# Down-sampled and local attention with a gated feed-forward layer on one core: first loads put in another order, small copies and products merged, and the list of steps drawn anew

## The chip, the cores and the metric

One Trainium2 chip, of which the program uses one core. The metric is device time in microseconds from start to end of the program, as the median over runs.

## The reference

For 8 batches of 8 heads, with 576 positions and 64 values a head, the reference makes two attentions and adds them: one over positions averaged by fours and repeated four times, and one over a band of seven keys. The sum, as 4608 tokens of 512 values, goes through a feed-forward layer with a gate.

```python
q_d, k_d, v_d = (t.reshape(B, H, S // 4, 4, D).mean(axis=3) for t in (q, k, v))
out_up = np.repeat(sm_attn(q_d, k_d, v_d), 4, axis=2)
mask = np.abs(pos[:, None] - pos[None, :]) < 4
attn = softmax(np.where(mask, scale * q @ k.transpose(0, 1, 3, 2), -1e9))
x = (out_up + attn @ v).transpose(0, 2, 1, 3).reshape(B * S, H * D)
y = (np.maximum(x @ w_gate, 0) * (x @ w_val)) @ w_out
```

## The kernel before

Two heads make a pair; there are 32 pairs, four to a batch. The tokens are cut in 9 chunks of 512. As soon as the pairs of a chunk's batch are done, the feed-forward products of that chunk run between the steps of the next pairs. Many of these products are made by schemes with seven products of half-size blocks in place of eight, with their sums on DVE.

PSUM is one tile, `ps`, of eight banks of 512 numbers. Each step names its bank.

The order of everything is written by hand: `SEQ` (L18) is a string of 2329 steps, and the loop at the end issues them one by one. Each engine runs its own instructions strictly in the order in which the list issues them; between engines, waits are put in from what each instruction reads and writes. A range of `ps` that an access spans counts as read, also where the access leaves banks out. So the list is at once the order of PE, ACT, DVE, POOL and SP.

A step is written kind/pair/arguments/bank. Those that matter here:

- `loadq`, `loadk`, `loadv` issue a pair's loads on POOL (L458, DMA rows at L467; L495, rows at L517). `cast` turns q of pair 0 to f16 on ACT.
- `tr/p/i/b` transposes a third of q and k of pair p on PE into bank b (`emit_flip2`, L547, matmuls L553, of half the array's width); it leaves 2 x 96 columns of each position and 2 x 48 of pooled ones there.
- `ev/p/i0X/b` copies the positions to `qkT` and `ev/p/i1X/b` the pooled columns to `qkd` (`emit_flipped`, L577, rows at L589), on ACT (X is A) or DVE (V).
- `s1` makes the scores on PE (L650 pooled, L661 in the band). They need `qkd` and `qkT`. `ed` and `ex` are their exponentials on ACT (L685, L671), `ma` the band's mask on DVE (L677).
- `vd`, `vc` pool v on PE (L631) and copy it on ACT (L640).
- `sd`, `su` are the products with v on PE (L698 and L710), `rd`, `ru` reciprocals of the sums of the exponentials on DVE (L722, L735), `td`, `tu` the normalising products on DVE (L727, L741): `tu` has two a pair, for three of the six blocks of 96 positions each.
- `xp`, `xe` transpose the result on PE (L928, L930) and copy it to `xT` (L940).
- `warm` and `brief` are matmuls on zeros that fill PE's time (L1115, L1125).
- From pair 4 on, `den` and `num` (L751, L760 and L772, L781, half the array's width) take the place of `sd`, `su` and what follows; from pair 8 on they are written `o/a...`, `o/b...`.
- `hg`, `hv` are whole-array products of the feed-forward layer (L945), `p`, `up`, `sq` blocks of the seven-product schemes (L1030, L1289, L1193), `next`, `sum`, `sumhi` their sums (L1024), `gate` and `gt` the gate (L957, L1384).
- POOL also adds parts of v for the later pairs (L602, L610).

Before the list starts, q of pair 0 is loaded through SP, the constants too, and twelve wide matmuls on zeros run on PE.

Of the kernel before, what the change touches and what calls it, by code (L numbers as in the profile page):

```python
# [12 lines left out]
ALU = mybir.AluOpType  # L13
# [5 lines left out]
qk/a0/0@6 cast tr/0/0/2 ev/0/00A/2 loadk/0 loadv/0 pads tr/0/1/3 ev/0/10A/3 ev/0/11A/3 tr/0/2/4 vd/0/6 ev/0/01A/2  # L19
loadq/1 loadk/1 loadk/3 ev/0/21V/4 loadv/1 tr/1/0/7 ev/0/20V/4 s1/0/2 loadq/2 loadk/2 vc/0/6 ev/1/00A/7 tr/1/2/1  # L20
tr/1/1/0 ev/1/01A/7 loadv/2 loadv/3 ed/0/2 warm/5/6 sd/0/6 loadq/3 loadk/4 wv/0 loadq/4 ex/0/0/2 brief/16/2 ev/1/21V/1
ev/1/20V/1 wg/0 loadk/5 ev/1/10A/0 loadv/4 rd/0/6 ma/0/0 ev/1/11A/0 loadk/6 s1/1/0 loadq/5 td/0/6 ex/0/1/2 ma/0/1
warm/2/7 ex/1/0/0 ma/1/0 su/0/4 ru/0/4 ed/1/0 vd/1/6 tr/2/0/0 ex/1/1/0 tr/2/2/3 tu/0/1/4 tu/0/0/4 tr/2/1/2 vc/1/6
ev/2/21V/3 ev/2/20V/3 ev/2/01A/0 ev/2/00A/0 ma/1/1 ev/2/11A/2 xp/0/1/5 xp/0/0/4 sd/1/6 xe/0/1V/5 ev/2/10A/2 s1/2/0
xe/0/0A/4 ex/2/0/0 ed/2/0 su/1/4 rd/1/6 td/1/6 warm/5/7 warm/1/7 vd/2/6 tr/3/0/0 ex/2/1/0 ma/2/0 ru/1/4 tu/1/1/4
tu/1/0/4 ma/2/1 tr/3/1/2 ev/3/00A/0 ev/3/01A/0 tr/3/2/3 ev/3/20V/3 ev/3/21V/3 warm/3/7 xp/1/1/5 xe/1/1V/5 ev/3/11A/2
vc/2/6 xp/1/0/4 sd/2/6 ev/3/10A/2 xe/1/0A/4 rd/2/6 td/2/6 s1/3/0 su/2/4 vd/3/6 ex/3/0/0 wg/1 loadv/5 ru/2/4 tu/2/1/4
tu/2/0/4 wv/1 hv/0/0/7 hv/0/1/7 ed/3/0 ex/3/1/0 tr/4/0/0 warm/4/1 ev/4/01A/0 wg/2 vc/3/6 xp/2/0/4 ev/4/00A/0 xe/2/0A/4
xp/2/1/5 ma/3/0 hv/1/0/1 loadq/6 loadk/8 loadk/7 loadv/6 ma/3/1 loadq/7 sd/3/6 hv/1/1/1 wv/2 xe/2/1V/5 su/3/4 rd/3/6
tr/4/2/3 tr/4/1/2 td/3/6 ev/4/11A/2 ev/4/10A/2 loadv/7 ru/3/4 tu/3/0/4 tu/3/1/4 hg/0/0/6 hg/0/1/6 hv/0/2/7 hg/1/0/0  # L30
wv/3 ones/6 ev/4/21V/3 loadq/8 ev/4/20V/3 wg/3 xp/3/1/5 xp/3/0/4 hv/1/2/1 hg/0/2/6 wo/1 xe/3/1V/5 wo/0 wo/2 xe/3/0A/4
s1/4/2 ex/4/0/2 hg/0/3/6 relu/0/6 hv/1/3/1 hv/0/3/7 hg/1/1/0 hg/1/2/0 hg/1/3/0 vd/4/6 ed/4/2 tr/5/0/2 tr/5/1/3
ex/4/1/2 tr/5/2/4 ev/5/01A/2 relu/1/0 vc/4/6 ev/5/10A/3 ev/5/11A/3 ev/5/00A/2 gate/0/7 ma/4/0 ma/4/1 hv/2/*/7 hg/2/*/6
relu/2/6 ev/5/20V/4 ev/5/21V/4 gate/1/1 den/4/1/5 den/4/0/4 ln/4 inv gate/2/7 num/4/1/3 num/4/0/2 xn/2 vd/5/1 hg/3/*/0
vc/5/1 s1/5/4 ex/5/0/4 hv/3/*/1 ex/5/1/4 ed/5/4 hg/4/*/2 hg/5/*/6 relu/3/0 relu/4/2 hv/4/*/3 ma/5/0 ma/5/1 tr/6/0/4
gate/3/1 xsum/4 gate/4/3 relu/5/6 tr/6/1/0 ev/6/00A/4 ev/6/11V/0 ev/6/01V/4 ones/4 num/5/0/2 den/5/1/5 tr/6/2/1
kk/a0/1@6 ev/6/10A/0 wo/3 num/5/1/3 qk/a2/0@6 qk/b1/0@0 den/5/0/4 kk/a1/1@6 const/0 const/1 v4/a/0@1 ln/4 inv
ev/6/21V/1 ev/6/20V/1 qk/a2/1@6 hv/5/*/7 gate/5/7 qk/b3/1@6 vd/6/1 vc/6/1 tr/7/1/0 s1/6/4 hg/7/*/1 xn/2 ev/7/11V/0
hg/8/*/2 hv/7/*/3 v/a/0@6 ex/6/1/4 ex/6/0/4 ma/6/0 ma/6/1 xsum/5 sum/2/0@1 ed/6/4 hg/6/*/7 v/a/1@6 relu/8/2 relu/7/1
gate/7/3 ev/7/10V/0 den/6/1/5 tr/7/2/1 tr/7/0/6 den/6/0/4 hv/8/*/0 relu/6/7 hv/6/*/7 num/6/0/2 ev/7/01V/6 gate/8/0  # L40
num/6/1/3 tr/8/2/0 ev/7/20A/1 loadv/8 qk/b0/0@0 qk/b1/1@0 qk/a0/1@0 qk/a3/1@0 qk/b3/0@0 qk/b2/0@0 qk/a2/1@0 qk/a1/0@1
qk/b0/1@0 qk/a1/1@0 v/a/1@0 v/b/0@0 qk/b2/0@1 qk/b2/1@0 qk/b3/1@0 gate/6/7 ln/4 inv ev/7/00A/6 ev/7/21A/1 s1/7/4
# [36 lines left out]
o/b10/0@2 o/b11/0@2 vh/7.1/0@2 next/2/0@2 gt/7.1.1/0@2 sq/2.2.0.6/1@2 up/0.1/1@2 ln/b0/0@2 inv/b/0@2 xn/b0/0@2
# [1538 lines left out]
```

## Time and profile before

| | us |
|---|---|
| median of 3 runs | 335.33 |
| the runs | 335.18, 335.33, 338.43 |
| the profiled execution | 334.61 |
| its span | 332.7 |
| PE's granted clock in it | 1.0 |

The span runs from the first to the last instruction of the profile. The rest of the profiled execution's time, 1.9 us, lies around it. In the rows, a start is in microseconds from the span's start, followed by the busy time of the group of like instructions; a matmul's end is modelled, so the starts are what tells how fast PE goes.

### The profile page before, as it was taken

How to read it: one execution, taken by the hardware profiler on the slowest of the kernel's cores; microseconds unless marked ns; L12 is line 12 of the kernel's file. 1: busy time of each engine (PE TensorE's matmuls, PEld its weight loads, DVE VectorE, ACT ScalarE, POOL GpSimd, SP SyncE). 2: the span in 40 equal slices, each digit the busy share in tenths (PEclk: the TensorE clock that was granted, in tenths of full speed). 3: DMA queues.
4: the chain of work that ended last, by engine and by line, in shares of the span. 5: the costliest groups of instructions: out<-in, count | busy, mean ns of one | idle time of the engine just before them, and what ended most of it. 6: DMA issues, size and time to landing. Idle time of an engine off the chain costs nothing.

```text
span 332.7 us, 9158 instructions
## 1 busy us (share of the span) xinstructions
PE 327.0 (98%) x3456; PEld 244.1 (73%) x3456; DVE 287.2 (86%) x574; ACT 268.3 (81%) x649; POOL 183.8 (55%) x268
## 2 busy tenths in 40 slices
PE   7999999999999999999999999999999999999996
PEld 3876556666577787778687868786878678888875
DVE  6795779999997989999999989979998998788792
ACT  4968887789988989899879989898889548787852
POOL 8864845928989788867974998845520000000000
PEclk9999999999999999999999999999999999999999
DMA  9999999999999999999999999999200102003024
GB/s 143 173 188 215 183 203 165 135 168 160 169 179 142 210 114 224 119 210 102 218 134 186 121 214 136 210 133 173 39 32 3 63 2 97 1 19 111 2 58 133
DMA packets 151808, 43.96 MB, mean 132 GB/s; under 512 B 136556, under 2 KB 146452, under 8 KB 151764
## 3 DMA queue, kind: packets, MB, share of 16 engines
q0 software_dynamic: 113344, 19.51, 79.1%
q1 hardware_dynamic: 38308, 23.83, 33.9%
q8 instruction: 27, 0.44, 0.6%
q14 instruction: 17, 0.14, 0.1%
q10 hardware_dynamic: 112, 0.04, 0.1%
HBM read 46.63 MB, written 9.44 MB: 169 GB/s over the span
## 4 chain that ended last, share of the span: by engine, by line
PE 95%; DMA 2%; DVE 1%; POOL 1%; issue 1%; ACT 1%; DVEq 0%; POOLq 0%
PE ps L945 30%; PE ps L1289 27%; PE ps L1193 18%; PE ps L1030 3%; PE ps L873 2%; PE ps L553 2%; PE ps L846 2%; PE ps L893 2%; DMA qk<-in_q_dram 2%; PE ps L888 1%; PE ps L842 1%; PE ps L631 1%; PE ps L661 1%; PE ps L650 1%; PE ps L751 1%; PE ps L772 1%
## 5 line engine op out<-in xcount | busy, mean ns | idle before, releaser
L945 PE MATMUL ps<-xT,wv_sb 128*128 128x512 f16 x352 | 90.0, 380 | 0.0
L945 PEld LDWEIGHTS <-wv_sb 128*128 128x128 f16 x352 | 32.7, 98 | 25.9
L472 POOL DMA_DIRECT2D qk<-in_k_dram x46 | 33.6, 734 | 16.7 <-DMA qkT<-qk 12.3
L1384 DVE SCALAR_TENSOR_TENSOR gT<-r,ps 128x512 f16<-128x512 f16 x55 | 37.3, 681 | 4.7 <-PE ps L945 3.8
L1289 PE MATMUL ps<-xT,qk 128*128 128x256 f16 x240 | 41.3, 272 | 0.0
L472 POOL DMA_DIRECT2D qk<-in_q_dram x46 | 34.0, 741 | 11.2 <-DMA qkT<-qk 4.6
L1289 PE MATMUL ps<-xT,wg_sb 128*128 128x256 f16 x180 | 33.8, 272 | 0.2 <-DVE xT L1307 0.2
L1300 ACT COPY ps<-ps 128x256 f32<-128x256 f32 x80 | 28.6, 365 | 5.7 <-PE ps L1289 4.8
L490 POOL DMA_DIRECT2D vw<-in_v_dram x40 | 28.9, 732 | 4.3 <-DMA qk<-in_q_dram 4.2
L540 DVE TENSOR_REDUCE qkd<-qkT 128x288 f16<-128x1152 f16 x23 | 30.8, 1341 | 0.0
L1204 ACT COPY ps<-ps 128x256 f32<-128x256 f32 x54 | 19.7, 370 | 12.7 <-PE ps L1193 11.4
L1289 PEld LDWEIGHTS <-qk 128*128 128x128 f16 x240 | 22.4, 97 | 7.4 <-issue 0.5
L610 POOL TENSOR_TENSOR vd<-v 48x192 f16<-48x192 f32 x40 | 25.8, 644 | 1.7
L945 PE MATMUL ps<-xT,wg_sb 128*128 128x512 f16 x104 | 26.6, 380 | 0.0
L1305 ACT CAST r<-ps 128x256 f16<-128x256 f32 x55 | 20.0, 372 | 7.8 <-PE ps L1289 6.8
L1289 PEld LDWEIGHTS <-xo 128*128 128x128 f16 x240 | 22.8, 98 | 3.3
L602 POOL TENSOR_TENSOR v<-v 112x384 f32<-112x384 f32 (+1 forms) x21 | 21.4, 1020 | 6.1 <-DMA v<-in_v_dram 5.6
L1289 PE MATMUL ps<-wt,xo 128*128 128x256 f16 x180 | 24.4, 273 | 0.0
L923 ACT ACTIVATE rden<-rden 128x720 f32<-128x720 f32 x28 | 22.5, 804 | 0.7
L957 DVE TENSOR_TENSOR gT<-r,ps 128x512 f16<-128x512 f16 x24 | 16.2, 680 | 6.7 <-ACT r L954 4.0
L1289 PEld LDWEIGHTS <-wg_sb 128*128 128x128 f16 x180 | 16.4, 97 | 6.5 <-issue 0.6
L1307 DVE TENSOR_TENSOR r<-ps,xT 128x256 f16<-128x256 f32 x44 | 17.3, 419 | 3.2 <-PE ps L1289 2.2
(175 smaller groups left out, 873.7 us busy)
## 6 DMA issues: line engine op xcount, KB each, us to landing
out_dram<-y_sb SPq DMA_DIRECT2D x24, 256.0 KB, 4.3
v<-in_v_dram SPq DMA_DIRECT2D x20, 192.0 KB, 5.3
qk<-in_q_dram POOLq DMA_DIRECT2D x46, 72.0 KB, 5.7
qk<-in_k_dram POOLq DMA_DIRECT2D x46, 72.0 KB, 6.0
vw<-in_v_dram POOLq DMA_DIRECT2D x38, 80.0 KB, 4.6
v<-in_v_dram SPq DMA_DIRECT2D x20, 144.0 KB, 5.5
out_dram<-y_sb SPq DMA_DIRECT2D x22, 128.0 KB, 1.8
vw<-in_v_dram POOLq DMA_DIRECT2D x12, 168.0 KB, 6.4
```

What stands on the lines that cost most here:

```text
L472: nc.gpsimd.dma_start(dst.rearrange("p (j h d) -> p j h d", h=2, d=64)[:, :, hh, :], _dap(src, off + hh * S * D, [[D, 96], [NQ * D, NB], [ ...
L490: nc.gpsimd.dma_start(t[lo : lo + 64, j0:j1, lo : lo + 64], _dap(v, base + j0 * QB * D, [[D, 64], [QB * D, j1 - j0], [1, D]]),)
L540: nc.vector.tensor_reduce(out=qkd[hp % 2].rearrange("p i t -> p (i t)"), in_=qkT[hp % 4][:, 0 : 2 * S].rearrange("p (t f) -> p t f", f=4), ...
L602: nc.gpsimd.tensor_tensor(out=m, in0=t[:, :, 0:128], in1=t[:, :, 128:256], op=ALU.add)
L610: nc.gpsimd.tensor_tensor(out=vp[hp % 3][lo : lo + 48, :, lo : lo + 64], in0=m[:, :, 0:64], in1=m[:, :, 64:128], op=ALU.add)
L923: nc.scalar.activation(out=rden, in_=rden, func=AF.Exp, scale=-1.0)
L945: nc.tensor.matmul(out=out, lhsT=w[:, kk, bass.ts(jj, 128)], rhs=xT[:, kk, c * TCH : (c + 1) * TCH], start=(kk == 0), stop=(kk == 3),)
L1193: nc.tensor.matmul(out=out, lhsT=self.left[i][t], rhs=self.right[i][t], start=(i == 1 and t == 0), stop=(t == n - 1), skip_group_check=True,)
L1289: nc.tensor.matmul(out=out, lhsT=self.left[i - 1][k], rhs=self.right[i - 1][k], start=(i == 1 and k == 0), stop=(k == n - 1), skip_group_c ...
L1300: nc.scalar.copy(out=o, in_=x)
L1305: nc.scalar.copy(out=o, in_=self.d if i == 11 else self.a)
L1384: lambda c, jj, b, t: nc.vector.scalar_tensor_tensor(out=gT[c % 2][:, jj, :], in0=tg[t], scalar=0.0, in1=ps[:, b, :], op0=ALU.max, op1=ALU ...
```

## The change

Three things are done to the steps, and the list is written anew around them.

The first loads: q of pair 1 goes ahead of v of pair 0, and the loads of pairs 1 to 3 follow in the order q, k, v (k of pair 3 stood among those of pair 1). `vd/0`, which reads v of pair 0, now stands behind the scores of pair 0.

The pooled copies on ACT of pairs 1, 2 and 3, `ev/p/01A` and `ev/p/11A`, become one, `eq/p/b0/b1`, which reads two banks in one access. In pair 1 the banks of the two first flips are swapped to 0 and 7.

The normalising products of pairs 0, 1 and 2, `tu/p/0` and `tu/p/1`, become one, `ta/p`, over all six blocks.

Matmuls, loads and what is computed are the same. The list has 2323 steps.

```diff
 SEQ = """
-qk/a0/0@6 cast tr/0/0/2 ev/0/00A/2 loadk/0 loadv/0 pads tr/0/1/3 ev/0/10A/3 ev/0/11A/3 tr/0/2/4 vd/0/6 ev/0/01A/2
-loadq/1 loadk/1 loadk/3 ev/0/21V/4 loadv/1 tr/1/0/7 ev/0/20V/4 s1/0/2 loadq/2 loadk/2 vc/0/6 ev/1/00A/7 tr/1/2/1
-tr/1/1/0 ev/1/01A/7 loadv/2 loadv/3 ed/0/2 warm/5/6 sd/0/6 loadq/3 loadk/4 wv/0 loadq/4 ex/0/0/2 brief/16/2 ev/1/21V/1
-ev/1/20V/1 wg/0 loadk/5 ev/1/10A/0 loadv/4 rd/0/6 ma/0/0 ev/1/11A/0 loadk/6 s1/1/0 loadq/5 td/0/6 ex/0/1/2 ma/0/1
+qk/a0/0@6 cast tr/0/0/2 ev/0/00A/2 loadk/0 loadq/1 pads tr/0/1/3 ev/0/10A/3 ev/0/11A/3 tr/0/2/4 ev/0/01A/2 loadv/0
+loadk/1 loadv/1 ev/0/21V/4 loadq/2 tr/1/0/0 ev/0/20V/4 s1/0/2 vd/0/6 loadk/2 loadv/2 ev/1/00A/0 vc/0/6 tr/1/2/1
+tr/1/1/7 loadq/3 loadk/3 ed/0/2 warm/5/6 sd/0/6 loadv/3 wv/0 loadk/4 loadq/4 ex/0/0/2 brief/16/2 ev/1/21V/1 ev/1/20V/1
+wg/0 loadk/5 ev/1/10A/7 loadv/4 rd/0/6 ma/0/0 eq/1/0/7 loadk/6 s1/1/0 loadq/5 td/0/6 ex/0/1/2 ma/0/1 warm/2/7 ex/1/0/0
...
-den/7/0/4 gate/10/6 zs/0.1/0@1 den/7/1/5 ln/4 inv next/0/1@0 num/7/1/7 tr/8/0/1 num/7/0/6 gate/11/0 next/1/1@0
...
+gate/9/1 next/0/1@0 wt/0 zero/b/6 vc/7/4 den/7/0/4 relu/11/7 num/7/1/7 den/7/1/5 next/1/1@0 gate/11/0 sumhi/0/0@1
+zero/k/0 p/1/0@1 num/7/0/6 ln/4 inv wt/1 tr/8/0/1 tr/8/1/0 p/2/0@1 p/5/0@1 keep/1/0@1 ev/8/01A/1 ev/8/10A/0
...
+    def emit_pooled_two(hp, b0, b1):
+        o = qkd[hp % 2].rearrange("p i t -> p (i t)")[:, 0:192].rearrange("p (b n t) -> p b n t", b=2, n=2)
+        nc.scalar.copy(out=o, in_=_sap(flat, (0, 128), 512 * b0 + 96, [[512 * (b1 - b0), 2], [240, 2], [1, 48]]))
...
+    def emit_tu_all(hp, bank):
+        nc.vector.tensor_tensor(
+            out=xo[hp % 3][:, 0:NB, :].rearrange("p j (h d) -> p h j d", h=2),
+            in0=_sap(ps, (0, 96), 512 * bank, [[513, 2], [65, NB], [1, 64]]),
+            in1=_sap(ru[hp % 2], (0, 96), 0, [[NB, 2], [1, NB], [0, 64]]),
+            op=ALU.mult,
+        )
...
+        "eq": emit_pooled_two,
...
+        "ta": emit_tu_all,
```

POOL's first loads, in the order before (`qk16_1` and `vw_1` are q and k, and v, of pair 1; the line of a row is that of the load):

```order
L467 DMA qk16_0_72<-in_k_dram 96x6x128
L517 DMA vw_0_82<-in_v_dram 112x12x64
L467 DMA qk16_1_73<-in_q_dram 96x6x128
L467 DMA qk16_1_73<-in_k_dram 96x6x128
L467 DMA qk16_3_75<-in_k_dram 96x6x128
L517 DMA vw_1_83<-in_v_dram 112x12x64
L467 DMA qk16_2_74<-in_q_dram 96x6x128
L467 DMA qk16_2_74<-in_k_dram 96x6x128
L517 DMA vw_2_84<-in_v_dram 112x12x64
L517 DMA vw_3_85<-in_v_dram 112x12x64
L467 DMA qk16_3_75<-in_q_dram 96x6x128
```

And now, from the same place (the lines of after are one lower here):

```order
L466 DMA qk16_0_72<-in_k_dram 96x6x128
L466 DMA qk16_1_73<-in_q_dram 96x6x128
L516 DMA vw_0_82<-in_v_dram 112x12x64
L466 DMA qk16_1_73<-in_k_dram 96x6x128
L516 DMA vw_1_83<-in_v_dram 112x12x64
L466 DMA qk16_2_74<-in_q_dram 96x6x128
L466 DMA qk16_2_74<-in_k_dram 96x6x128
L516 DMA vw_2_84<-in_v_dram 112x12x64
L466 DMA qk16_3_75<-in_q_dram 96x6x128
L466 DMA qk16_3_75<-in_k_dram 96x6x128
L516 DMA vw_3_85<-in_v_dram 112x12x64
```

q of pair 1 and v of pair 0 change places; k of pair 1 is the fourth in both. k of pair 3 goes from fifth to tenth.

ACT from the copy of pair 0's pooled v on, before, with the engines that a row waits for in brackets (`qkT_90` and `qkd_94` belong to pair 1, L685 and L671 are `ed` and `ex`):

```order
L640 CAST vd_96<-ps 72x2x2x64 [waits PE_49]
L589 CAST qkT_90<-ps 128x384 [waits PE_49]
L589 CAST qkd_94<-ps 128x96
L685 ACTIVATE att<-ps 72x2x2x144 [waits DVE_49,PE_49]
L671 ACTIVATE att<-ps 112x2x288
L589 CAST qkT_90<-ps 128x384 [waits PE_49]
L589 CAST qkd_94<-ps 128x96
L671 ACTIVATE att<-ps 112x2x288
L671 ACTIVATE att<-ps 112x2x288 [waits DVE_49,PE_49]
```

And now (L595 is `eq`):

```order
L588 CAST qkT_90<-ps 128x384 [waits PE_49]
L643 CAST vd_96<-ps 72x2x2x64 [waits PE_49]
L688 ACTIVATE att<-ps 72x2x2x144 [waits DVE_49]
L674 ACTIVATE att<-ps 112x2x288
L588 CAST qkT_90<-ps 128x384 [waits PE_49]
L595 CAST qkd_94<-ps 128x192 [waits DVE_49,PE_49]
L674 ACTIVATE att<-ps 112x2x288
L674 ACTIVATE att<-ps 112x2x288 [waits PE_49]
```

The first copy of 96 columns is gone, the second is 192 wide and has waits of its own, on DVE and on PE; the copy of pair 0's pooled v moved behind pair 1's first.

446 lines of the change are left out of this document (222 added, 224 removed).

## The prediction

> **What bounds the kernel now.** I read the page's head first, then the waits of PE, then the stretches of the start and of one busy stage.
>
> ```profile
> span 332.7 us, 9158 instructions
> PE 327.0 (98%) x3456; PEld 244.1 (73%) x3456; DVE 287.2 (86%) x574; ACT 268.3 (81%) x649; POOL 183.8 (55%) x268
> PE 95%; DMA 2%; DVE 1%; POOL 1%; issue 1%; ACT 1%; DVEq 0%; POOLq 0%
> ...
> PE ps L1115 <- DVE zero_sb L430: 1.3, 1, 1.3
> PE ps L631 <- DMA vw<-in_v_dram: 0.5, 1, 0.5
> PE ps L553 <- DMA qk<-in_q_dram: 0.3, 1, 0.3
> PE ps L1289 <- DVE xT L1307: 0.2, 1, 0.2
> ```
>
> The first three lines are the page's, the last four are everything that PE waited for by the view of waits. PE is busy for 327.0 of 332.7 us, it carries 95% of the chain, and three of its four waits lie in the first 9 us. The order of after holds the same 3456 matmuls. So the change can win at most what PE waits for, 2.3 us by these rows, of which the first 1.3 (the memset of the zero tile) is untouched; and it can lose whatever the new order makes PE wait. ACT and DVE are shares of 81 and 86%: a copy saved on them is worth nothing unless PE stood behind it.
>
> **The loads.** POOL issues the first loads, here its timeline, with the DMA view of one short stretch, PE's timeline, and one piece of the chain of waits:
>
> ```profile
> 2.20 0.96 POOL L517 DMA_DIRECT2D vw<-in_v_dram  x1
> 3.14 0.73 POOL L467 DMA_DIRECT2D qk<-in_q_dram  x1
> 3.86 1.45 POOL L467 DMA_DIRECT2D qk<-in_k_dram  x2
> ...
> qk<-in_k_dram POOLq DMA_DIRECT2D x1, 144.0 KB, 5.3
> ...
> 7.50 0.49 PE L631 MATMUL ps<-vw,cst_sb 112*128 112x128 f16 x6 [0.54 <-DMA vw<-in_v_dram]
> 8.33 0.44 PE L553 MATMUL ps<-gT,qk 96*64 96x144 f16 x8 [0.34 <-DMA qk<-in_q_dram]
> 9.21 0.69 PE L553 MATMUL ps<-gT,qk 96*64 96x144 f16 x16
> ...
> 3.14 5.15 DMA qk<-in_q_dram
> ```
>
> v of pair 0 is issued at 2.20 and ends PE's wait at 7.50; q of pair 1 is issued at 3.14, takes 5.15 and lands at 8.29; k of pair 1, the fourth load, is issued at 3.86 and, by the 5.3 of the DMA view, lands at 9.16. The change swaps v of pair 0 and q of pair 1, so tr/1/0 can start some 0.9 us earlier (issue at 2.20 instead of 3.14) and vd/0 comes 0.7 later, by the issue time of one q load. But both orders have the same four loads ahead of tr/1/2, the x16 row at 9.21, and k of pair 1 stays the fourth. It landed 0.05 before that row began. So PE's waits of 0.5 and 0.3 only move to other places before 9.2: I take 0.0 for the load order, with 0.05 as the most that it can win. The later swaps bring v of pair 1, q and k of pair 2 forward and k of pair 3 back; none of them ended a wait of PE before, so they are nothing as well.
>
> **The merged copy of pair 1.** ACT had two copies of 96 columns, ev/1/01A right behind tr/1/0 and ev/1/11A at 10.75. Now there is one of 192 columns, eq/1/0/7, which reads banks 0 and 7 in one access, a range that takes in all eight banks. The order shows new waits on it, for DVE and PE: what the program holds it for are the reciprocal rd/0 (bank 6) and the last of brief/16 (bank 2), the work on banks in between that stands ahead of it in the list. ACT, PE and DVE from 10.3 to 13.6, by the timeline:
>
> ```profile
> 10.39 0.48 ACT L589 CAST qkT<-ps 128x384 f16<-128x384 f32 x1
> 10.75 0.26 ACT L589 CAST qkd<-ps 128x96 f16<-128x96 f32 x1
> 10.88 1.48 ACT L671 ACTIVATE att<-ps 112x576 f16<-112x576 f32 x2
> ...
> 10.62 0.74 PE L1125 MATMUL ps<-zero_sb 128*128 128x80 f16 x16
> 11.29 0.25 PE L650 MATMUL ps<-qkd 64*72 64x144 f16 x2
> ...
> 10.89 0.18 DVE L722 RECIPROCAL rd<-ps 72x4 f32<-72x4 f32 x1 [0.48 <-PE ps L698]
> ...
> 11.71 0.21 ACT att L671
> ...
> 13.44 0.04 issue
> 13.48 0.69 PE ps L553 x16
> ```
>
> Before, the scores s1/1 (L650) followed brief/16 without a pause, at 11.29, since their pooled operand was ready at 11.01. Now the copy cannot start before brief/16 ends at 11.36 (10.62 + 0.74); the reciprocal, done at 11.07, is earlier. How long it takes no row shows: of the ACT copies here, the 96-wide one takes 0.26 and the 384-wide one 0.48, so 192 columns lie between; I take 0.33, on the line through both. With 0.05 at either end (13.44 to 13.48 is such a step) it runs from 11.40 to 11.73, and s1/1 starts at 11.78: 0.5 us later, in which PE stands still. The last three rows, the chain's, show what follows: exp of s1/1 starts 0.42 behind it (11.71), then ed/1, the second exp, and tr/2/2 on PE at 13.48, whose bank that exp frees. All of it moves by the same 0.5. On ACT the exp ex/0/1 stands queued behind the copy and starts about 0.7 later than 10.88; ma/0/1 on DVE and the second half of su/0 on PE wait for it, but they have the 0.2 to 0.3 that PE lost ahead of tr/2/2 anyway. I take +0.5. The ends are 0, if the copy is let go before brief/16 ends, and +0.7, if ex/0/1 decides.
>
> **The other merged instructions.** The copies of pairs 2 and 3 read banks 0 and 2 with nothing foreign between; each is still released by the flip that released the second copy before, and saves about 0.1 of ACT ahead of a full queue. The products ta/0 to ta/2 replace two of 384 elements each on DVE:
>
> ```profile
> 13.02 1.02 DVE L741 TENSOR_TENSOR xo<-ps,ru 96x384 f16<-96x384 f32 x2
> 14.10 0.30 PE L928 MATMUL ps<-cst_sb,xo 72*128 72x288 f16 x1
> ```
>
> Both products end at 14.04, and PE reaches xp/0/1 at 14.10 after the flips of pair 2, which set its start; one instruction of the same 768 elements saves at most the second one's fixed part, and the flips are now later too. Behind the products of pairs 1 and 2 PE has idle matmuls (warm) to fill the gap. So: 0, and no more than 0.1 either way.
>
> **The redrawn list.** PE pays for each change between matmuls of the whole array and those of a half (den, num, s1, flips). PE's timeline at two such changes:
>
> ```profile
> 77.84 1.03 PE L945 MATMUL ps<-xT,wg_sb 128*128 128x512 f16 x4
> 78.70 0.82 PE L1030 MATMUL ps<-wt,xo 128*128 128x256 f16 x6
> ...
> 85.73 1.03 PE L945 MATMUL ps<-xT,wg_sb 128*128 128x512 f16 x4
> 86.69 0.32 PE L772 MATMUL ps<-att,vw 112*64 112x96 f16 x6
> 87.23 0.23 PE L760 MATMUL ps<-att,ones_sb 72*64 72x72 f16 x4
> 87.30 0.29 PE L751 MATMUL ps<-att,ones_sb 112*64 112x288 f16 x2
> 87.42 0.23 PE L760 MATMUL ps<-att,ones_sb 72*64 72x72 f16 x4
> 87.58 1.04 PE L945 MATMUL ps<-xT,wv_sb 128*128 128x512 f16 x4
> ```
>
> From start to start four L945 take 0.86 where L1030 follows (77.84 to 78.70) and 0.96 where the half-array L772 follows: 0.10 to go in. Four L760 take 0.07 within a stretch (87.23 to 87.30) and 0.16 at its end: 0.09 to come out. The old list keeps num and den of a pair in one stretch. The new one splits pairs 7 and 8 (six full matmuls p/1/0@1 stand between num/7/1 with den/7 and num/7/0, and likewise for pair 8): two more stretches, 2 x 0.19 = +0.4. The Trainium skill, "TensorEngine Tiling (Array Packing)", Key Properties, has the rule: changing the tiling mode drains TensorE. By "TensorE: Matmul & The Clock Gate", Single matmul latency, the warm drain and issue of one matmul is about 166 ns, so an estimate by that page is 4 x 0.166 = 0.7, and the sum would be 0.3 higher. The rows above price it at less.
>
> What else moves after 25 us are places in the queues of ACT, DVE and PE. The one wait there shows what such a queue can cost:
>
> ```profile
> 136.41 1.00 POOL L602 TENSOR_TENSOR v<-v 112x384 f32<-112x384 f32 x1
> 136.58 1.25 DVE L1024 TENSOR_TENSOR xo<-gT 128x768 f16<-128x768 f16 x1
> 137.64 0.38 PE L1289 MATMUL ps<-xT,wg_sb 128*128 128x256 f16 x2
> 137.75 0.41 DVE L1307 TENSOR_TENSOR xT<-ps,xT 128x256 f16<-128x256 f32 x1
> 138.22 0.38 PE L1289 MATMUL ps<-xT,wg_sb 128*128 128x256 f16 x2 [0.20 <-DVE xT L1307]
> L1024 DVE TENSOR_TENSOR xo<-gT,xo 128x768 f16<-128x768 f16 x12 | 6.6, 550 | 0.1
> ```
>
> A sum of 0.55 us took 1.25 while POOL added, the product behind it came late, and PE stood: two matmuls began at 137.64, the next at 138.22. At 0.11 each (the x6 row at 78.70: 0.27 for the last of six, so 0.55 for the other five) it was due at 137.86 and came 0.4 late, of which the view counts 0.20 as idle. That wait may go or another may come; I take 0 for the list beside the stretches, between -0.4 and +2.
>
> **Sum.** Against the profiled execution (334.6 us, span 332.7 and 1.9 around it): 0 for loads, +0.5 for the copy, 0 for the other merges, +0.4 for the stretches: +0.9. The median of the three runs, 335.33, lies 0.7 above that execution; I add the sum to it: 336.2. For this kernel about 1%, 3.4 us, is what I count as a change; 0.9 is none.
>
> **Rivals.** *The start gets shorter.* The chain of waits itself names the q load, with the issue of v ahead of it, so a reader may expect the 0.8 us of waits back, and the merges to count where ACT and DVE are full. For the merges speaks the price of a small copy: 0.26 for 96 columns against 0.48 for 384 leaves 0.19 that does not depend on size, and three ACT copies and three DVE products less would be about 1 us in all. "VectorE: DVE Perf Modes", the section on the TRN2 errata, in the Trainium skill says the same as a rule: every instruction pays a fixed latency, a large one pays it once. By it the kernel gains. Against: k of pair 1 at 9.16, and that none of the merged instructions but eq/1 stands at the end of a wait. If it holds and the copy does not wait, -0.8 to -1.8 + 0.4 gives 333.9 to 334.9. Chance 12%.
>
> *DVE falls behind POOL (slower).* The collision of 136.58 costs PE 0.4 where DVE's queue has no slack. POOL makes such sums for every later pair (L602, L610), and the new list moves DVE's sums against them. To leave "no change" it takes 3.4 - 0.9 = 2.5 us, six such stalls of 0.4 where the old list had one; at ten it gives 335.33 + 0.9 + 4.0 = 340.2. The rule is in the Trainium skill, "Trainium Architecture — The Big Picture", What this means for kernel authors: VectorE and GpSimd share a port pair by an exclusive lock. The row agrees. Against it: one in 300 us before, and POOL's own order is the same. Chance 8%.
>
> *The change does nothing to PE:* the copy's wait is over in time and the list wins back its stretches, 335.0 to 335.6, 15%. My forecast, 335.6 to 338.0, has the remaining 65%.
>
> **Range and chances.** 334.8 to 338.0 holds the forecast, the case of nothing and the upper edge of the gain; what is left out is most of the first rival and the collisions, 18%. Faster by over 1% would need 3.4 us where PE waits for 2.3 in all: 2%. Slower by over 1% is the second rival: 8%. Within 1%: 90%.
>
> **What would show it.** Right: PE's waits name ACT qkd at L653 near 11.7 us with about 0.5; the 192-wide copy at L595 starts right after brief/16; the x16 flips of pair 1 still start near 9.2; PE is solid after 15 us and its last matmul starts about 0.9 later than before. Wrong: the copy runs at 10.6 and s1/1 at 11.3 (no start loss), flips of pair 1 well ahead of 9.2 (the loads count), or new PE waits for DVE of 0.3 and more between 40 and 250 us (the collisions).

## The result, and the profile after

| | median us | executions | ratio to the kernel before, 95% interval |
|---|---|---|---|
| kernel before, beside the changed one | 336.20 | 12 | |
| changed kernel | 338.25 | 12 | 1.0068 [1.0045, 1.0090] |
| profiled execution before | 334.61 (span 332.7) | 1 | |
| profiled execution after | 338.40 (span 336.6) | 1 | |

The changed kernel is 0.68% slower, 2.3 us by the ratio (2.05 by the medians); 336.2 and at most 338.0 were forecast. The two profiled executions lie 3.9 us of span apart: that of before was one of its quickest (over all its runs here its times go from 334.2 to 338.4), so the traces overstate the difference.

The page of the changed kernel (its span, engines and chain), and all that PE waited for by the view of waits (total, times, longest):

```profile
span 336.6 us, 9146 instructions
PE 329.0 (98%) x3456; PEld 244.0 (73%) x3456; DVE 290.3 (86%) x571; ACT 269.2 (80%) x646; POOL 185.3 (55%) x268
PE 88%; DVE 7%; DMA 1%; issue 1%; POOL 1%; ACT 0%; DVEq 0%; POOLq 0%
...
PE ps L1126 <- DVE zero_sb L429: 1.3, 1, 1.3
PE ps L1300 <- DVE y_sb L1318: 1.0, 2, 0.9
PE ps L552 <- DMA qk<-in_k_dram: 0.5, 1, 0.5
PE ps L653 <- ACT qkd L595: 0.4, 1, 0.4
PE ps L956 <- DVE xn L919: 0.4, 1, 0.4
PE ps L552 <- DMA qk<-in_q_dram: 0.3, 1, 0.3
PE ps L884 <- DVE gT L1395: 0.3, 1, 0.3
```

PE is still busy 98% of the span with the same 3456 products, but DVE now carries 7% of the chain, where it carried 1. The wait for the merged copy (L595) is there, and three kinds of waits for DVE that the kernel before did not have. Waits for DMA are as long as before, 0.8.

The start, from PE's and ACT's timeline (start, duration, engine, line, operation, and in brackets the idle time before it):

```profile
7.07 0.44 PE L552 MATMUL ps<-gT,qk 96*64 96x144 f16 x8 [0.34 <-DMA qk<-in_q_dram]
7.97 0.49 PE L634 MATMUL ps<-vw,cst_sb 112*128 112x128 f16 x6
8.94 0.69 PE L552 MATMUL ps<-gT,qk 96*64 96x144 f16 x16 [0.48 <-DMA qk<-in_k_dram]
...
10.35 0.74 PE L1136 MATMUL ps<-zero_sb 128*128 128x80 f16 x16
11.13 0.32 ACT L595 CAST qkd<-ps 128x192 f16<-128x192 f32 x1 [0.80 <-PE ps L1136]
11.50 0.26 PE L653 MATMUL ps<-qkd 64*72 64x144 f16 x2 [0.41 <-ACT qkd L595]
```

The first flips of pair 1 start 1.26 earlier (7.07, 8.33 before), its sixteen others at 8.94 instead of 9.21, behind k of pair 1. The copy starts when brief/16 ends (10.35 + 0.74 = 11.09) and takes 0.32. The scores s1/1 start at 11.50, 1.15 after brief/16 began; before, that distance was 0.67 (10.62 to 11.29). So the copy costs 0.48 there. The 0.27 at the sixteen flips is no gain of the load order: over all traces kept here they start at 8.92 to 9.49 with the old loads (eight traces) and at 8.94 to 9.57 with the new ones (twelve).

The largest of the new waits, from the timelines of POOL, DVE and PE near 173 us:

```profile
170.11 1.00 POOL L605 TENSOR_TENSOR v<-v 112x384 f32<-112x384 f32 x1
172.84 1.00 POOL L605 TENSOR_TENSOR v<-v 112x384 f32<-112x384 f32 x1
...
170.16 1.37 DVE L1035 TENSOR_TENSOR xo<-gT,xo 128x768 f16<-128x768 f16 x1
173.31 0.95 DVE L1035 TENSOR_TENSOR xo<-gT 128x768 f16<-128x768 f16 x1
174.18 0.41 DVE L1318 TENSOR_TENSOR y_sb<-ps,q 128x256 f32<-128x256 f32 x1
...
173.39 0.38 PE L1300 MATMUL ps<-xT,qk 128*128 128x256 f16 x2
174.65 0.82 PE L1300 MATMUL ps<-xT,gT 128*128 128x256 f16 x6 [0.87 <-DVE y_sb L1318]
```

Two sums of 0.55 on DVE took 1.37 and 0.95, each beside a sum on POOL; DVE's next result, which frees a bank, came at 174.59, and PE's next products started at 174.65. They were due at 173.61 (173.39 and two products of 0.11), 1.04 earlier.

The view of waits lists long waits only. To see the short ones I took, for each product of PE, the distance to the start of the next and subtracted its own columns at 2.4 per ns (four products of 512 columns start 0.86 apart in all), half of that where two half-array products run side by side (four of 72 columns start 0.07 apart in all, 87.23 to 87.30 in the prediction's rows). What is left is PE's lateness; its sum grows from 19.4 to 23.3 us, by the 3.9 that the last product starts later (329.20 and 333.10). By stretch, with four kernels of the experiments below (before_tiny_sums, after_tiny_sums, tiny_no_eq1 and after_clear):

| us | before | after | before, sums cut | after, sums cut | the same, no merged copy of pair 1 | after_clear |
|---|---|---|---|---|---|---|
| 0–20 | 5.97 | 6.18 | 5.96 | 6.60 | 6.04 | 6.31 |
| 20–50 | 3.31 | 3.32 | 3.31 | 3.47 | 3.31 | 3.34 |
| 50–90 | 2.96 | 3.48 | 2.95 | 3.44 | 3.57 | 3.46 |
| 90–110 | 0.64 | 1.59 | 0.53 | 1.29 | 1.16 | 1.38 |
| 110–250 | 4.52 | 6.40 | 4.26 | 4.39 | 4.48 | 5.23 |
| 250 to the end | 2.03 | 2.37 | 2.00 | 2.33 | 2.30 | 2.35 |
| sum | 19.4 | 23.3 | 19.0 | 21.5 | 20.9 | 22.1 |

### The profile page after: what moved, and what is told of

Read it like the earlier page. It is cut to its first block, busy times and chain, and to the rows that moved or that the text cites. A ratio compares the mean times of both kernels' runs of the same rounds, so it can differ in the third digit from the quotient of the medians.

```text
span 336.6 us, 9146 instructions
## 1 busy us (share of the span) xinstructions
PE 329.0 (98%) x3456; PEld 244.0 (73%) x3456; DVE 290.3 (86%) x571; ACT 269.2 (80%) x646; POOL 185.3 (55%) x268
## 4 chain that ended last, share of the span: by engine, by line
PE 88%; DVE 7%; DMA 1%; issue 1%; POOL 1%; ACT 0%; DVEq 0%; POOLq 0%
PE ps L956 28%; PE ps L1300 23%; PE ps L1204 18%; PE ps L1041 3%; PE ps L884 2%; PE ps L552 2%; DVE xo L1035 2%; PE ps L857 2%; DMA qk<-in_k_dram 1%; DVE gT L1395 1%; PE ps L904 1%; PE ps L899 1%; DVE r L1318 1%; PE ps L853 1%; PE ps L634 1%
## 5 line engine op out<-in xcount | busy, mean ns | idle before, releaser
L471 POOL DMA_DIRECT2D qk<-in_k_dram x46 | 33.6, 732 | 20.9 <-DMA qkT<-qk 17.0
L1300 PE MATMUL ps<-xT,qk 128*128 128x256 f16 x240 | 42.0, 272 | 0.0
L1311 ACT COPY ps<-ps 128x256 f32<-128x256 f32 x80 | 28.5, 365 | 6.3 <-PE ps L1300 5.0
L1300 PE MATMUL ps<-xT,wg_sb 128*128 128x256 f16 x180 | 33.0, 272 | 0.1
L1215 ACT COPY ps<-ps 128x256 f32<-128x256 f32 x54 | 19.4, 368 | 13.1 <-PE ps L1204 10.6
L1318 DVE TENSOR_TENSOR r<-ps,xT 128x256 f16<-128x256 f32 x44 | 17.9, 418 | 4.6 <-PE ps L1300 2.5
```

Source lines behind the costliest of these rows:

```text
L471: nc.gpsimd.dma_start(dst.rearrange("p (j h d) -> p j h d", h=2, d=64)[:, :, hh, :], _dap(src, off + hh * S * D, [[D, 96], [NQ * D, NB], [ ...
L1300: nc.tensor.matmul(out=out, lhsT=self.left[i - 1][k], rhs=self.right[i - 1][k], start=(i == 1 and k == 0), stop=(k == n - 1), skip_group_c ...
L1311: nc.scalar.copy(out=o, in_=x)
L1318: nc.vector.tensor_tensor(out=o, in0=self.b if i == 12 else self.a, in1=self.m, op=ALU.add)
```

## Experiments

The theories were: **start** (the time is lost before some 25 us), **collisions** (VectorE's f16 sums stand still while GpSimd adds v, and the new list has more or worse of it) and **list** (the redrawn order itself makes PE wait, collisions or not). The expectations also name a **switch** theory: the list costs no more than its two added stretches of half-array products, 0.4. "before" in a ratio is always the kernel before, run in turns beside the experiment. Its median in these groups of runs goes from 335.36 to 335.78 (336.20 beside the changed kernel), so times of different groups that are less than some 0.4 apart say little by themselves.

**1. Where along the list.** Both lists hold the same steps ahead of s1/4/2 of pair 4, up to those that the change merges. So the first part of one list can be joined to the rest of the other.

```diff
 new_start_old_list:  new list up to s1/4/2, then the old one
 old_start_new_list:  old list up to s1/4/2, then the new one
```

> The changed kernel's first steps (loads, pair 1's merged copy, the merged products, up to the step s1/4/2 of pair 4), then the old list word for word. Against the kernel before, in us. Start theory (the extra time is lost before about 25 us): +1.5 to +2.5. Collision theory (VectorE's f16 sums stand still while GpSimd adds v, and the redrawn list after the start has more or worse of these): +0.2 to +0.6, the sum of PE's starts being late by 0.2 at 20 us in the trace of the changed kernel. Switch theory (the two stretches of half-array products that the list adds): +0.2 to +0.6 as well, since they lie behind the splice.

> The reverse: the old first steps with separate copies, products and the old order of loads, then the new list from s1/4/2 on. Against the kernel before, in us. Start theory: 0 to +0.3. Collision theory: +1.3 to +2.3, with PE waits for VectorE results again between 90 and 260 us. Switch theory: +0.4 from two stretches of half-array products and nothing else, no new waits for VectorE.

Measured: 336.31, ratio 1.0023 [1.0006, 1.0041], for the new start; 337.94, ratio 1.0072 [1.0056, 1.0087], for the new list behind the old start. The start costs some 0.8 us, and the list behind it about 2.4, as much as the whole change within the intervals. (Together they are more than the 2.3 of the change; each interval is about 0.5 us wide to either side.) The start theory falls.

**2. GpSimd's sums cut to one column, in both kernels.** The instructions and their waits stay, the pooled v is left out of the output (in all kernels below whose name begins with tiny as well).

```diff
-nc.gpsimd.tensor_tensor(out=m, in0=t[:, :, 0:128], in1=t[:, :, 128:256], op=ALU.add)
+nc.gpsimd.tensor_tensor(out=m[:, :, 0:1], in0=t[:, :, 0:1], in1=t[:, :, 128:129], op=ALU.add)
...
-in0=m[:, :, 0:64], in1=m[:, :, 64:128]
+in0=m[:, :, 0:1], in1=m[:, :, 0:1]
```

> The kernel before with GpSimd's sums of v (L602, L610) cut to one column each: the same number of instructions in the same places, but the pooled v is left out of the output. Collision theory: VectorE's sums at L1024 and L868 are never over 0.6 us, and the time falls by 0.3 to 1.2 us, since VectorE's trace of before has eight collisions worth 3.1 us of which one of 0.4 reached PE in the profiled run. Start and switch theories: the same time as before within 0.3.

> The changed kernel with the same cut of GpSimd's sums (pooled v left out of the output). Collision theory: no VectorE sum over 0.7 us, PE's waits for VectorE between 90 and 260 us gone, 1.5 to 2.5 us faster than the changed kernel, so at most 0.9 slower than the kernel before with the same cut (start 0.2 to 0.5 and two stretches 0.4). Start theory: as slow as the changed kernel, +2 against before. Switch theory: the gap to the kernel before with the same cut stays at +2.

Measured: before with the cut 334.03, 0.9958 [0.9943, 0.9973]; after with the cut 336.40, 1.0021 [1.0006, 1.0036]. DVE's sums at this line, grouped by operands (minimum, median and maximum in ns), in the changed kernel without and with the cut:

```profile
L1035 DVE TENSOR_TENSOR xo<-gT x30: 210/550/1356, 41.9 to 249.6; 128x768 f16<-128x768 f16 x18, 128x640 f16<-128x640 f16 x6, 128x128 f16<-128x128 f16 x6
L1035 DVE TENSOR_TENSOR xo<-gT,xo x12: 547/552/1371, 60.4 to 256.7; 128x768 f16<-128x768 f16 x12
```

```profile
L1035 DVE TENSOR_TENSOR xo<-gT x30: 215/547/572, 42.5 to 247.8; 128x768 f16<-128x768 f16 x18, 128x640 f16<-128x640 f16 x6, 128x128 f16<-128x128 f16 x6
L1035 DVE TENSOR_TENSOR xo<-gT,xo x12: 546/550/557, 61.0 to 254.9; 128x768 f16<-128x768 f16 x12
```

The maximum falls from 1371 to 572 ns, so it is POOL's work that stretches them, and the four long waits of PE for DVE that the trace of after has between 102 and 211 us (2.4 us of lateness together) are gone. But the kernel before gains as much from the cut (335.78 to 334.03, 1.75 us by the medians, 1.4 by the ratio) as the changed one (1.85 and 1.6): the two, run in turns with the cut, stay 2.4 apart (2.1 by the ratios). Collisions cost both kernels about the same; in the median they are not what sets them apart. That part of the collision theory falls, against what the trace of after alone suggests.

**3. Three suspects in the new list, one at a time and together.** All with the sums cut, where the times scatter less.

```diff
 tiny_joined
-p/1/0@1 num/7/0/6            ... o/a00/0@1 hg/1/0@1 o/a10/0@1
+num/7/0/6 p/1/0@1            ... o/a00/0@1 o/a10/0@1 hg/1/0@1
 tiny_no_eq1
-eq/1/0/7
+ev/1/01A/0 ev/1/11A/7
 tiny_zero_early
-xsum/b/1@1 zero/b/3 relu/5/1@1 zero/b/4
+inv/a/1@1 zero/b/3 ... gate/3/1@1 zero/b/4 ... xsum/b/1@1 relu/5/1@1
```

> The changed kernel with GpSimd's sums cut to one column (pooled v left out of the output) and two steps moved, so that the half-array products of pairs 7 and 8 run in as few stretches as in the old list: num/7/0/6 ahead of p/1/0@1, hg/1/0@1 behind o/a10/0@1. The same kernel without the move took 336.4 (ratio 1.0021 to the kernel before). Stretch theory: 0.3 to 0.5 us faster than that, two places with 0.10 going in and 0.11 coming out fewer in PE's starts between 54 and 67 us. If the work is only shifted: no difference.

> The changed kernel with GpSimd's sums cut to one column, and pair 1's merged copy (eq/1/0/7) replaced in its place by two copies of one bank each. Prediction's mechanism (the merged copy waits for every bank between 0 and 7): the copies start at about 10.8 instead of 11.2 us, PE's wait of 0.58 for them before s1/1 falls to 0.2 or less, 0.3 to 0.5 us faster than 336.4. Rival (the wait is for the flips of pair 1, which the loads bring late): the wait stays and the extra copy adds 0.1.

> The changed kernel with GpSimd's sums cut to one column, and the steps zero/b/3 and zero/b/4 (ScalarE's copies of zeros, L838, four of 0.46 us that the new list puts at 92 to 94.5 us) moved up to where the old list has them, behind inv/a/1@1 and behind gate/3/1@1. ScalarE theory: PE's seven waits of about 0.1 for L1311 between 96 and 106 us go, 0.5 to 0.8 us faster than 336.4. If ScalarE only carries its backlog from elsewhere: under 0.2.

> The three moves together, GpSimd's sums cut to one column. If they add up: 1.1 to 1.8 us faster than 336.4, so 334.6 to 335.3, which leaves 0.6 to 1.3 us to the kernel before with the same cut (334.03). If what is removed comes back in the next wait: within 0.5 of 336.4.

Measured, against 336.40: tiny_joined 336.26, tiny_no_eq1 335.83, tiny_zero_early 337.21, tiny_all_three 336.66 (ratios to before 1.0011 [0.9997, 1.0025], 1.0003 [0.9988, 1.0017], 1.0037 [1.0023, 1.0051] and 1.0023 [1.0009, 1.0037]).

The copy of pair 1 is worth 0.57 by the medians. PE's and ACT's timeline of tiny_no_eq1 at that place:

```profile
10.70 0.73 PE L1136 MATMUL ps<-zero_sb 128*128 128x80 f16 x16
10.89 0.39 ACT L588 CAST qkd<-ps 128x96 f16<-128x96 f32 x2
11.36 0.25 PE L653 MATMUL ps<-qkd 64*72 64x144 f16 x2
```

The two copies run while brief/16 still writes its bank, and s1/1 follows the 16 products without a pause: it was the reach over the banks between, and not the flips, that held the merged copy. In every trace kept here s1/1 starts 1.14 or 1.15 after brief/16 began where the copy is merged, and 0.66 or 0.67 after it where it is not, the kernel before included. With full sums edits_no_eq1 (in 4) and new_start_old_list differ in this copy alone: 1.0003 and 1.0023 of the kernel before.

Joining took 0.14 instead of 0.4, too little to tell from no gain: of the two stretches only that of pair 8 went. With num of pair 7 moved up, the flips behind it became a stretch of their own. The number of changes between products of the whole array, of half its columns and of half its rows is 59 in after_tiny_sums, 57 here, 56 in the kernel before. In the trace the lateness at the changes between 43 and 95 us falls by 0.20, but the whole lateness only by 0.03: PE waited elsewhere instead.

The zeros were put in the wrong place, ahead of products that still read that buffer (the result of that pair changes too), and PE waited for them. ACT's and PE's timeline:

```profile
90.29 0.93 ACT L838 COPY vw<-zero_sb 64x320 f32<-64x320 f32 x2
...
91.27 0.32 PE L783 MATMUL ps<-att,vw 112*64 112x96 f16 x6 [0.68 <-ACT vw L838]
```

That run says nothing about ACT's load, and tiny_all_three contains it. It was repeated in 5.

**4. Middle or late, and the edits alone.**

```diff
 tiny_new_middle:  old list to const/1, new to sq/4.0.0.3/0@2 (about 100 us), then old
 tiny_new_late:    old list to sf/4.0.0.22/0@2, then new
 edits_no_eq1:     new start with ev/1/01A/0 ev/1/11A/7 for eq/1/0/7, then old list; full sums
```

> GpSimd's sums cut to one column. The old list up to const/1, then the new list up to the compute step sq/4.0.0.3/0@2 (about 25 to 100 us; loads that the two lists have on different sides of the seam are issued at the seam), then the old list again. The kernel before with the same cut took 334.03, the changed one 336.4. If the redrawn list loses its time in this middle part (PE's waits for ScalarE between 86 and 100 us, one more stretch of half-array products left): +0.8 to +1.4 over 334.03. If it loses it later: under +0.4.

> GpSimd's sums cut to one column. The old list up to sf/4.0.0.22/0@2, the new list from there on (about 100 us to the end). If the middle part has the loss: +0.3 to +0.6 over 334.03, from a wait of 0.23 near 258 us for a VectorE sum (L1318) and waits of 0.07 to 0.18 for ScalarE's copies. If the late part has it: +1.0 to +1.7.

> Full sums. The changed kernel's start (new order of loads, merged products of pairs 0 to 2, merged copies of pairs 2 and 3) with pair 1's copy kept as two, then the old list. Against the kernel before: within 0.3 if only pair 1's merged copy and the redrawn list behind the start cost time; +0.5 or more if the loads or the merged products cost something of their own.

Measured: tiny_new_middle 335.36, 0.9998 [0.9986, 1.0011]; tiny_new_late 334.98, 0.9989 [0.9974, 1.0003]; edits_no_eq1 335.44 beside 335.42 for before, 1.0003 [0.9983, 1.0022]. Over the 334.03 of before with the cut, the middle costs 1.3 and the late part 0.95 (1.3 and 1.0 by the ratios). They add up to more than the 1.8 that is left of the changed kernel without eq/1 (335.83 - 334.03), because the seams bring waits of their own: tiny_new_middle has one of 0.41 for DVE at 99.5 us, just behind its seam, and tiny_new_late one of 0.29 near 289, and neither is in the whole list. So the loss is spread, most of it ahead of 110 us, as the table of lateness shows too. The edits without pair 1's copy cost nothing that can be told from zero (the interval is 0.6 us wide to either side): loads, three merged products and two merged copies are 0.0.

**5. The short waits for ScalarE.** In after_tiny_sums PE is late by 0.06 to 0.18 six times between 96 and 106 us (0.66 together), five times behind a copy of ACT (L1311) by the trace. One of them, ACT and PE by the timeline, and then PE at the same kind of place in before_tiny_sums:

```profile
95.72 0.72 ACT L838 COPY att<-zero_sb 128x640 f32<-128x640 f32 x1
96.35 0.37 ACT L1311 COPY ps<-ps 128x256 f32<-128x256 f32 x1
...
96.00 0.82 PE L1300 MATMUL ps<-wo_sb,gT 128*128 128x256 f16 x6
96.77 0.38 PE L1300 MATMUL ps<-xT,qk 128*128 128x256 f16 x2
...
94.97 0.82 PE L1289 MATMUL ps<-wo_sb,gT 128*128 128x256 f16 x6
95.63 0.60 PE L1289 MATMUL ps<-xT,qk 128*128 128x256 f16 x4
```

Six products of 0.11 that start at 96.00 would let the next start at 96.65; the copy ends at 96.72, and it is 96.77. No bracket stands there: the modelled end of the six covers the gap. In before_tiny_sums the products behind the same six start 0.66 after them (94.97 to 95.63), on time, and between 96 and 106 us none of its products comes over 0.04 late. Two ways to have that copy earlier were tried:

```diff
 tiny_zero_ln:    zero/b/3 behind inv/a/1@1, zero/b/4 behind ln/b/1@1
 tiny_act_order:  exp/a0/0@2 zero/k/1 kk/b1/0@2 uk/2.1/0@2 (ACT), mask/a0/0@2 ed/a/0@2 in the old list's places
```

> The changed kernel with GpSimd's sums cut to one column; zero/b/3 behind inv/a/1@1 and zero/b/4 behind ln/b/1@1, where the old list has them, so that ScalarE's copies of zeros no longer stand at 92 to 94.5 us. If they hold up the copies behind them: PE's waits for L1311 between 96 and 106 us fall from 0.66 to under 0.35, and the time by 0.3 to 0.6 from 336.4. If not: the waits stay and the time is 336.4 within 0.2.

> The changed kernel with GpSimd's sums cut to one column; exp/a0/0@2, mask/a0/0@2, zero/k/1, kk/b1/0@2, uk/2.1/0@2 and ed/a/0@2 put among their neighbours where the old list has them, PE's order of products left as it is. If the order of ScalarE's steps makes the waits: those at 96.5, 97.8 and 98.3 us (0.30 together) go and the time falls by 0.2 to 0.4 from 336.4. If PE's own order makes them: no change, or the wait comes back at another copy.

Measured: tiny_zero_ln 336.39, 1.0031 [1.0019, 1.0044], no change. The wait before 96.77 went, and one of 0.17 for a DVE sum came at 99; together the waits between 96 and 106 us are 0.66 as before. tiny_act_order 337.09, 1.0057 [1.0042, 1.0073], 0.7 slower. ACT and PE there:

```profile
99.47 0.36 ACT L1311 COPY ps<-ps 128x256 f32<-128x256 f32 x1
...
99.89 0.38 PE L1300 MATMUL ps<-wt,xo 128*128 128x256 f16 x2 [0.62 <-ACT ps L1311]
```

With ACT's steps in the old order and PE's products in the new one, a copy that PE needs stands behind others and PE waits 0.62. So these steps of ACT can't be put back alone. Which of the moved products makes the short waits was not found.

**6. With full sums: the copy, and the meetings taken apart.**

```diff
 after_no_eq1:    eq/1/0/7 as two copies
 before_split:    first sum of v on GpSimd as one instruction per slice; before_split_both: the second as well
 after_clear, at @4 and @5:
-sum/2 sum/3 ... gt/10.6.1 ... pool/b ... next/0/0      v2/a ... v1/a after/3
+sum/2 gt/10.6.1 ... sum/3 next/0/0 ... pool/b          after/3 v2/a v1/a
 before_clear, at @2 to @5:  after/3 v2/a v1/a
```

> The changed kernel with full sums, pair 1's merged copy as two copies in its place. With the column cut this move gave 0.57 us. If it is as much here: 337.6 to 337.8, 1.5 to 1.9 slower than the kernel before. If the collisions of VectorE and GpSimd later take up what the start gives: 338.0 to 338.4.

> The changed kernel, nothing left out. At the two places (near 173 and 210 us) the steps gt/10.6.1 and next/0/0 go up behind sum/2 and sum/3, so that VectorE's sums stand together as in the old list, and GpSimd's sums v2/a and v1/a go behind the step that waits for them (after/3/0). Collision theory: PE's waits of 1.04 and 0.53 there go, the time falls by 1.0 to 1.5 from 338.25, to 336.7 to 337.3. If the list has another reason for being late there (PE ahead of VectorE for lack of slack): the waits stay above 0.3 each, time 338.0 to 338.5.

> The kernel before with each first sum of v on GpSimd (L602, 1.03 us) as three or four instructions of one slice, nothing left out. If a VectorE f16 sum waits for the end of GpSimd's running instruction alone, its stalls shrink from up to 0.8 to at most about 0.3 us, and the time falls by 0.3 to 1.0 of the 1.75 that cutting the sums saved. If it waits until GpSimd is idle, no change; if the extra instructions make v late, slower.

> The kernel before with both of GpSimd's sums of v in slices (the first by its three or four slices, the second, of the later pairs, by its three), nothing left out. If a VectorE sum waits only for the end of the instruction that runs: its stalls are at most 0.3 instead of 0.8, the time falls by 0.5 to 1.2 us. If it waits until GpSimd is idle, as the first sum's slices alone leave open: no change.

> The kernel before with v2/a and v1/a of GpSimd behind the step after/3/0 in all four waves, nothing left out. If the meetings with VectorE's sums near 137 us and its like reach PE in most executions: 0.3 to 0.8 faster than the kernel before. If later sums then meet others: no change.

Measured: after_no_eq1 337.96, 1.0078 [1.0062, 1.0094]: no gain that can be told from the changed kernel. In its trace s1/1 follows brief/16 without a pause, as in tiny_no_eq1, but there is a wait of 0.49 for a DVE sum at 239.6 that the trace of after lacks. A gain at the start may be lost again where the shifted work meets POOL; one trace doesn't show that, nor how often.

after_clear 337.18, 1.0042 [1.0023, 1.0061], 1.1 faster than the changed kernel. DVE and POOL by the timeline (the lines of this kernel are one higher: L1036 is L1035), and PE's waits:

```profile
171.04 0.55 DVE L1036 TENSOR_TENSOR xo<-gT,xo 128x768 f16<-128x768 f16 x1
171.51 0.55 DVE L1036 TENSOR_TENSOR xo<-gT 128x768 f16<-128x768 f16 x1
171.98 1.34 DVE L540 TENSOR_REDUCE qkd<-qkT 128x288 f16<-128x1152 f16 x1
...
172.06 0.99 POOL L606 TENSOR_TENSOR v<-v 112x384 f32<-112x384 f32 x1
```

```profile
PE ps L1127 <- DVE zero_sb L430: 1.3, 1, 1.3
PE ps L885 <- DVE gT L1396: 0.7, 1, 0.7
PE ps L553 <- DMA qk<-in_k_dram: 0.7, 2, 0.4
PE ps L654 <- ACT qkd L596: 0.4, 1, 0.4
PE ps L553 <- DMA qk<-in_q_dram: 0.2, 1, 0.2
```

The sums run in 0.55 each, and the POOL sum lies beside the reduction, which takes its usual 1.34. The waits of 1.04 and 0.53 near 173 and 210 us are gone (both are in the traces of after and after_no_eq1, and old_start_new_list has their like). The edit also moves two steps of DVE's own, gt/10.6.1 and next/0/0, so how much of the 1.1 is POOL's alone isn't separated. The 0.7 for gT in the list is another meeting, at 116.7 us, where a DVE sum took 2.00 in this execution.

In the old list neither moving POOL's sums nor slicing them helps: before_clear 335.94, 1.0002 [0.9979, 1.0025]; before_split 334.94, 0.9997 [0.9981, 1.0013]; before_split_both 336.00, 1.0019 [1.0003, 1.0035]. In the trace of the last the longest DVE sum of this line falls to 0.93 us, but more of them are touched: of the 62 sums of 768 columns eleven take over 0.6 us, where four do in the trace of before, and one of another line takes 1.04. No version with the sums whole is shown to beat the kernel before.

## Why the prediction was off

- **The base.** The sum was put on 335.33, the median of three runs; beside the changed kernel the kernel before took 336.20. So 0.9 of the way from the forecast 336.2 to 338.25 is the base. On 335.33 the measured ratio gives 337.6, inside the range; that the time came out above 338.0 is in part bad luck with the base. The change itself was forecast at +0.9 and is +2.3.
- **Load order, 0.0: held.** k of pair 1 stays the fourth load, and its landing ends the wait of the x16 flips, at 8.94. Over the traces their start is the same with both orders within its scatter, and edits_no_eq1, with the new loads and without pair 1's merged copy, runs as the kernel before does.
- **Merged copy, +0.5: held.** It waited for brief/16, took 0.32 (0.33 assumed) and put s1/1 off by 0.48; with the sums cut it is worth 0.57, and ahead of the old list with full sums 0.7 (new_start_old_list against edits_no_eq1, by the ratios). That it can be won back in the full changed kernel isn't shown (after_no_eq1).
- **Other merges, 0: held**, by edits_no_eq1 again.
- **Two more stretches of half-array products, +0.4: the price is right.** The new list has four more changes between whole and half products (56 instead of 52; 59 instead of 56 with those between half rows and half columns). Lateness at changes between 43 and 95 us grows from 2.44 to 2.85 with the sums cut. That a stretch can be had back is not shown (tiny_joined). The rule of the Trainium skill ("TensorEngine Tiling (Array Packing)", Key Properties) that a change of tiling drains the array is seen here at 0.09 to 0.10 going in and 0.11 to 0.13 coming out.
- **"I take 0 for the list beside the stretches": this is the term that failed.** It is the mis-sized one, though its ends, -0.4 and +2, hold what it measured. 335.83 - 334.03 = 1.8 us (1.5 by the ratios) is what the redrawn list costs behind the start with neither collisions nor the merged copy, and 0.4 of it is the stretches. The other 1.4 are waits too short for the view of waits. The traces of before_tiny_sums and tiny_no_eq1 say the same: beyond 20 us their lateness differs by 0.41 at changes and by 1.38 elsewhere. Of that, some 0.7 is for ACT's copies between 86 and 106 us, 0.23 for a DVE result at 258, 0.11 for one at 76, the rest in pieces under 0.1. I had read the list for the one long wait it had, and had no row for short ones, since the old list has hardly any (0.53 of lateness between 90 and 110 us against 1.16 in tiny_no_eq1). Which change of the order makes them stays open.
- **The rival "DVE falls behind POOL": its mechanism is real, its part in the difference is not shown.** The trace of after looks like it, with four late results, the sign that the prediction named for it. It would have been wrong to stop there: with the sums cut the two kernels are as far apart as before. after_clear shows that two of the meetings, with the moved DVE steps, cost the new list 1.1 us. The old list loses about as much to the meetings, by what the cut saved, and not always at the same places: its products are late for DVE by 0.4 at 138 us in the trace of before, at 138 and 186 us in that of edits_no_eq1, and at 186 us alone in that of new_start_old_list (0.3). The Trainium skill, "SBUF — State Buffer", the section on the two sides of SBUF, states which operations it concerns: a VectorE operation with two inputs in SBUF (against one of GpSimd that reads SBUF), or in a two-port mode, and one of GpSimd exclude each other for a whole instruction. The traces agree on which: the f16 sums are held, while sums that read one input from PSUM (L1318) never take over 0.43, 37 of them beside a sum of POOL in the trace of after, and the reduction beside a POOL sum stays at 1.34.
- **The rival "the start gets shorter"** got nothing that can be told from the scatter of the loads, and the copy cost 0.48. **The rival "nothing happens to PE"** was wrong by the 2.3.

Sum of what the runs showed, with the sums cut: 0.6 for the copy, 0.4 for the stretches, 1.4 for short waits: 2.4, which is the 336.40 - 334.03 between the two kernels (the 1.4 is what is left of it, and is borne out by the lateness alone). The forecast had the first two and added nothing for the third.

## What to carry to other kernels

Where one engine is busy 98% and its order is written by hand, a redrawn order is not neutral until shown: many waits of 0.1 us don't appear in a view of waits, and the distance from start to start on the full engine finds them. Before blaming a mechanism that the trace of the slower kernel shows, take it out of both kernels; here it cost both about the same. And a merged access must not reach over banks that are still being written.

## What the hardware showed that was not expected

- A DVE f16 sum of 0.55 that starts while POOL adds ends 0.42 after POOL's instruction does: 170.16 to 171.53 and 173.31 to 174.26, with POOL's sums ending at 171.11 and 173.84. These two meetings cost 0.82 and 0.40.
- A DVE sum that starts first is saved in most rows. In the traces of before, after and after_clear six such sums began ahead of POOL's, and five of them took 0.55. POOL and DVE in the trace of after:

```profile
100.66 1.30 POOL L605 TENSOR_TENSOR v<-v 112x384 f32<-112x384 f32 x1
...
100.56 0.55 DVE L1035 TENSOR_TENSOR xo<-gT,xo 128x768 f16<-128x768 f16 x1
```

  Here it is POOL's sum that is stretched, to 1.30 from its usual 1.00. The sixth row, in after_clear, reads otherwise:

```profile
115.84 1.44 POOL L490 DMA_DIRECT2D vw<-in_v_dram  x2
117.27 1.03 POOL L606 TENSOR_TENSOR v<-v 112x384 f32<-112x384 f32 x1
...
116.73 2.00 DVE L1036 TENSOR_TENSOR xo<-gT,xo 128x768 f16<-128x768 f16 x1
```

  The DVE row begins 0.54 ahead of POOL's sum, behind which it ends by the same 0.43. By the Trainium skill, "SBUF — State Buffer", the section on the two sides of SBUF, the one that starts first keeps the ports. The five rows agree, this one does not. POOL's issuing of loads, which runs to 117.28, does not explain it alone: 25 other sums of this size in that trace lie beside nothing of POOL's but such issues, and none takes over 0.56. The cause of this row stays open.
- Cutting POOL's sums into their slices does not help: before_split_both has a longest sum of 0.93 at this line instead of 1.25, and is not faster than the kernel before (1.0019 [1.0003, 1.0035]).
